# A fused attention and feed-forward kernel: the fourth chunk's tokens are transposed on TensorE in place of the DMA, and the weight scaling and the attention ranks move with it

## The chip, the cores and the metric

The kernel runs on one core of one Trainium2 chip. The metric is device time in microseconds (us) of one execution. Before the change three runs took 210.88, 211.31 and 212.09 us; the median is 211.31 us.

## What is computed

Attention with a window of 128 tokens and 4 always visible first tokens (sinks), over 4 batches, 8 heads, 768 tokens and 64 values per head. The heads are put side by side into tokens of 512 values, and a feed-forward layer with a norm and a residual follows.

```python
scores = scale * np.matmul(q, k.transpose(0, 1, 3, 2))
keep = is_sink | in_window            # first 4 keys, or 0 <= i - j < 128
a = softmax(np.where(keep, scores, -1e9))
x = np.matmul(a, v)                   # heads side by side: (4, 768, 512)
xn = (x - mu) / np.sqrt(var + 1e-06) * g_ln
out = x + np.maximum(xn @ w_ch1, 0.0) @ w_ch2    # 512 -> 2048 -> 512
```

The inputs and the output are fp32; the kernel multiplies in bf16.

## The kernel before, in words

**Tiles and chunks.** The 3072 tokens are 24 tiles of 128 (t = 0 to 23) and 12 chunks of 256 (c = 0 to 11, two tiles each, three chunks per batch). For each chunk the kernel transposes q and k, computes the attention of its two tiles, normalises the tokens, transposes them (`xnt`) and runs the two layers of the feed-forward part.

**Transposes of q and k** (`chunk`, line 674). Chunks 0 to 3 (`c < by_dma`, 4) are transposed by matmuls with an identity (`by_pairs`, L618 and L625). From chunk 4 on POOL issues loads that cast to bf16 (L724), and SP issues DMA transposes (`dma_t`, L597). Line 727 puts the q transposes of chunk 5 and later behind the DMA transpose, on SP, of the second tile of the chunk two before (`trx_op[2 * c - 3]`), where that transpose exists. `gate` and `gate_v` (lines 590 to 594) hold back POOL's loads of k, q and v from chunk 5 on until a certain tile's norm (`rs_op`) is done.

**Attention.** Chunks 0 to 2 use `attend_tile` and `attend`; from tile 6 on `block(t)` (line 941) is one job of TensorE: the values of tile t-1 (L981, L988, L997) and the scores of tile t (L1008, for an even tile also the sinks, L1016). ACT takes the exponential (L1026, L1036), DVE multiplies by the band of the window (L1031). DVE then divides the values by the softmax sum (L1049, L1051).

**Norm** (`normalise`, line 899). DVE: mean and variance (L902, L904). POOL: variance plus 1e-6, to the power -0.5, two instructions (L912, L913). In chunks 0 to 2 `xc` is x minus the mean (L909, waits for no POOL result; the factor is put in at the end). From chunk 3 on (`by_seven`) `xc` is also multiplied by POOL's result (L916), so it waits for it. Then the tokens are transposed. For chunks below `x_by_dma` (3) TensorE transposes, four matmuls per tile into one PSUM bank (L924), and DVE or ACT moves them out and multiplies by the norm's weight g (L935, or four instructions on ACT, L936). From chunk `x_by_dma` on SP issues one DMA transpose per tile (L926, L597), and g has to be in w1 already.

**The scaling of w1** (lines 1260 to 1268). Behind the first layer of chunk `x_by_dma - 1` the four slices of w1 are multiplied by g in place: 16 instructions, on DVE (L1266) or ACT (L1267). Each waits for the last matmul that uses the unscaled slice (`last_use`), and the first layer of later chunks waits for the scaled slice (`Bw1g`, line 1071).

**Feed-forward** (`mlp`, line 1056). The first layer is eight jobs of 8 matmuls (L1067), each followed by a relu (L1078 on ACT, L1080 on DVE). The second layer is a plain product for chunks 0 to 2 (`second`, L1214). From chunk 3 on `second_by_seven` (line 1087) makes it from seven products instead of eight: DVE forms sums of relu results (L1095), TensorE multiplies (L1118), ACT copies parts out (L1125) and frees the bank that the next product writes, DVE adds up (L1129, L1159).

**What sets the order.** Nothing is written in order by hand. Each job is given to a planner (`Plan`) with its engines and cost in us, its rank (`prio`), and what it reads and writes. `Plan.run` (line 116) goes through time: of the jobs whose start lies within a window of the earliest possible start on that engine (0.3 us on TensorE, 0.25 on ACT, DVE and POOL), it takes the one of lowest rank. The result is one fixed order per engine, in which the chip waits for semaphores. Costs that matter here: POOL's two norm instructions 0.88 us; scaling one piece of w1 0.26 us on DVE and 0.065 + 0.000833 x 512 = 0.49 us on ACT; from one engine to another 0.035 us, to TensorE 0.11. `lat` (line 108) adds a lateness from `PAR["late"]` where TensorE waits for a DMA of a given name, if it is planned behind 30 us.

**Ranks.** First layer of chunk c: 16c + 8.5 to 16c + 15.5. Second layer: from 16c + 16.5 on. Block t of chunk c: `d = at(c, "blk") + step * i - lead[min(c, 5)]` with `at(c, "blk")` = 16c - 16 and i = 0 or 1 (line 943). TensorE transposes of tokens: 16c + 1 + i. So before the change block 6 ranks 30, block 7 40, block 8 43, block 9 53, block 10 55 (its values, a job of its own, 51), block 11 65.

Of the kernel before, what the change touches and what calls it, by code (L numbers as in the profile page):

```python
# [65 lines left out]
class Plan:  # L66
# [41 lines left out]
    def lat(self, src, dst):  # L108
        if src.eng == "PE" and src.dma is None:
            return -self.PE_DRAIN if dst == "PE" else self.SEM  # L110
        late = PAR["late"].get(src.name[:3], 0.0) if src.dma is not None and src.start > 30.0 and dst == "PE" else 0.0
        return late + (self.TO_PE if dst == "PE" else self.SEM)

    WINDOW = {"PE": 0.3, "ACT": 0.25, "DVE": 0.25, "POOL": 0.25, "SP": 0.0}

    def run(self):
# [8 lines left out]
        while ready:  # L125
# [4 lines left out]
            for o in ready:  # L130
                if "PE" in o.engs and o is not head and o.prio >= PAR["strict"]:
                    continue
# [66 lines left out]
def pe(us):  # L199
    return {"PE": (us, us + Plan.PE_DRAIN)}  # L200
# [7 lines left out]
def dve(n, per=1.04):  # L208
    t = 0.067 + 0.001 * per * n
    return (t, t + 0.09)  # L210


def fix(occ, extra=0.09):
    return (occ, occ + extra)
# [18 lines left out]
NEVER = -1e9  # L233
BIG = 3.3e38

PAR = dict(late={"trx": 1.25, "trk": 2.0, "trq": 2.0}, solo={10: 4.0}, bh=12, k_nb={(5, "k", 0): 53.0, (5, "k", 1): 53.0, (5, "q", 0): 53.0, (5, "q", 1): 53.0}, vs1=33.0, s4=2.0, w2t_pool=0, cut=(1, 2), rs_nb={4: 48.0, 5: 48.0}, v_nb={8: 49.0, 9: 52.0}, last7=1, opool=0, gk=(5, 4), gv=(4, 5), strict=400.0, win=0.4, tr=-8.0, sc=-5.0, sc1=-2.0, av=2.0, blk=-8.0, step=10.0, trx=9.0, by_dma=4, x_by_dma=3,
           w1p=(1.6, 2.6, 2.7, 2.8), pm=3, w2p=(4.5, 4.51, 4.52, 4.53), apart=2, vs0=(2.0, 13.0), by_tile=0, vp=(0.0, 0.1, 2.0, 2.1, 4.55, 4.56), ld1=0.05, t0=0.8, warm=7.9, pm0=-40.0, w1g=17.0, gtt=1.25, seven=3, lead=(0, 0, 0, 2, 5, 9), w2t=-4.0, at7=(0.5, 1.5, 2.5, 3.5, 4.5, 6.5, 7.5))


def general(tc, nc, slots, pairs, ones, ident_f, ident, w1, w2, mhalf, g_s, g_r, q, k, v, out, scale):  # L240
# [133 lines left out]
def kernel(  # L374
# [24 lines left out]
    NC = B * RC  # L399
# [70 lines left out]
    def constant(name, eng, us, prio, emit, reads=(), **kw):  # L470
        return P.op(name, {eng: fix(us)}, prio, emit, reads=[Bc[r] for r in reads], **kw)
# [46 lines left out]
    def negs(e):  # L518
# [27 lines left out]
    for b in range(B):  # L546
        n_vs = 4 if b else H
        P.op(f"vs{b}", {"DVE": dve(260)} if b else {"POOL": (0.9, 1.0)}, PAR["vs0"][0] if b == 0 else PAR["vs1"] - 12 if b == 1 else 48.0 * b - 20, lambda e, b=b, n=n_vs: (V if b else G).tensor_tensor(
            vs[b], vc[:, b, :].unsqueeze(1).to_broadcast([128, n, 65]),
# [21 lines left out]
    def at(c, step):  # L571
        return 16.0 * c - 8.0 + PAR[step]
# [11 lines left out]
    def early(t):  # L584
        return 0.5 + 0.8 * t

    rs_op, trx_op = {}, {}
    natf_users, natp_users = [], []

    def gate(c):  # L590
        return [rs_op[2 * c - PAR['gk'][c > 5]]] if PAR["by_dma"] < c < NC else []

    def gate_v(c):
        return [rs_op[2 * c - PAR['gv'][c != 5]]] if PAR["by_dma"] < c <= NC else []

    def dma_t(dst, src):
        nc.sync.dma_start_transpose(out=dst, in_=src)  # L597
# [54 lines left out]
    def load_m(t, prio):  # L652
        b, r = min(t, NT - 1) // RB, t % RB
        m = vn_b[t] = Buf(f"v{t}", "vn")
        at = lambda t0, s0, n, hs: v[t0, hs, s0:s0 + n, :].rearrange("h p d -> p h d")
        lo, hi, s0 = slice(0, 4), slice(4, 8), 128 * r
        parts = []
        if r:
            parts = [(0, 128, hi, at(b, s0 - 64, 128, hi)), (0, 64, lo, at(b, s0, 64, lo)), (64, 64, lo, at(b, s0 - 64, 64, lo))]
        else:  # L660
            pb = (t - 1) // RB
            parts = [(0, 64, hi, at(pb, S - 64, 64, hi)), (64, 64, lo, at(pb, S - 64, 64, lo))]
            if t < NT:
                parts += [(64, 64, hi, at(b, 0, 64, hi)), (0, 64, lo, at(b, 0, 64, lo))]
        for i, (p0, n, hs, src) in enumerate(parts):
            P.op(f"vld{t}_{i}", {"POOL": (0.8, 0.85)}, prio + 0.001 * i, lambda e, p0=p0, n=n, hs=hs, src=src: G.dma_start(  # L666
                m.t[p0:p0 + n, hs, 0:64], src), writes=[m], dma=SW_H if n == 128 else SW_Q, after=list(ones_of.values()) + gate_v(t // 2), nb=PAR["v_nb"].get(t, 0.0))
# [6 lines left out]
    def chunk(c):  # L674
        b, R = c // RC, c % RC
        d = at(c, "tr") if c >= 2 else early(2 * c)
        ld = d - 14.0 if c >= RC else 4.0
        if c < 2:
            kT_b[c], qT_b[c] = Buf(f"kT{c}", "kT"), Buf(f"qT{c}", "qT")
            if c == 0:  # L680
                nats = [Buf("kf", "natf"), Buf("qf", "natf")]
                for hh in range(2):
                    hs = slice(4 * hh, 4 * hh + 4)
                    for i, (x, T) in enumerate(((k, kT_b[c]), (q, qT_b[c]))):
                        nm, src, part = "kq"[i], nats[i], Buf(f"{'kq'[i]}l{hh}")
                        ap = x[b, hs, 0:256, :].rearrange("h (p i) d -> p h (i d)", i=2)
                        P.op(f"{nm}ld{hh}", {("SP" if i == 0 else "ACT"): (0.53, 0.53)}, -70 + hh,
                             lambda e, src=src, ap=ap, hs=hs: (nc.sync if e == "SP" else nc.scalar).dma_start(
                                 src.t[:, hs].rearrange("p h i d -> p h (i d)"), ap), writes=[src, part], dma=HW_F)
# [558 lines left out]
    w2t = [[flat_f[0][:, m] for m in range(2)], [flat_f[1][:, m] for m in range(2)], flat_p[0:2], flat_p[2:4]]  # L1248
# [114 lines left out]
```

## Time and profile before

| | |
|---|---|
| Median of three runs | 211.31 us (210.88 to 212.09) |
| The profiled execution, its own time | 210.67 us |
| Its span, first to last instruction | 209.2 us |
| Mean granted TensorE clock | 0.997 of full speed |
| DMA | 27.82 MB in 104557 packets, mean 133 GB/s |

In the profile PE is TensorE's matmuls, PEld its weight loads, DVE VectorE, ACT ScalarE, POOL GpSimd and SP SyncE; SPq and POOLq are the queues that issue DMAs. A group's line has the source line, the engine, the operation, output and input tile, the shapes and the count; behind the bar stand the busy time in us, the mean of one in ns, and the idle time of the engine just before, with what ended it. A line of a timeline has start and length in us. Matmuls overlap, so the time that one costs is read from the start of the next group and not from its own length. Since TensorE works through one fixed order, its idle time in a stretch, and what ended it, is the first thing to look for.

### The profile page before, as it was taken

The page shows a single profiled execution, that of the slowest core. Times are in us where ns is not written, and L with a number is a line of the kernel's source. Part 1 is how long each engine was busy: PE and PEld are TensorE (multiplying, and loading weights), DVE is VectorE, ACT ScalarE, POOL GpSimd, SP SyncE. Part 2 cuts the span into 40 slices and gives each one's busy share as a digit, 9 for nine tenths or more (in the row PEclk, how much of TensorE's full clock was granted, in tenths as well). Part 3 has the DMA queues.
Part 4 walks back from the last instruction along what each step waited for, and adds up shares of the span by engine and source line. Part 5 has one row for each costly group of instructions (what it writes and reads, how often), then busy time and mean ns, then how long its engine had stood idle before and what let it go on. Part 6 is the DMA issues. An engine that isn't in the chain of part 4 may idle for free.

```text
span 209.2 us, 7213 instructions
## 1 busy us (share of the span) xinstructions
PE 201.6 (96%) x2969; PEld 170.0 (81%) x2971; DVE 158.5 (76%) x427; ACT 122.2 (58%) x214; POOL 116.2 (56%) x170
## 2 busy tenths in 40 slices
PE   7899999999999799999999999999999999999992
PEld 2558865688888688888888888888888888888881
DVE  5699865899897778787778788778778678673472
ACT  3798677153897176385665664665664764453610
POOL 7969842479989974757694693694632202410000
PEclk9999999999999999999999999999999999999998
DMA  5999999999999999999999999999992220220202
GB/s 154 191 186 200 190 208 203 171 180 130 151 184 133 144 170 135 120 207 127 100 153 155 109 135 161 132 154 143 145 173 51 78 75 5 81 73 0 103 25 85
DMA packets 104557, 27.82 MB, mean 133 GB/s; under 512 B 93764, under 2 KB 101576, under 8 KB 104520
## 3 DMA queue, kind: packets, MB, share of 16 engines
q0 software_dynamic: 70960, 13.18, 92.1%
q1 hardware_dynamic: 32360, 13.35, 38.9%
q10 hardware_dynamic: 1200, 0.79, 1.3%
q8 instruction: 24, 0.39, 0.9%
q14 instruction: 13, 0.11, 0.2%
HBM read 27.43 MB, written 6.29 MB: 161 GB/s over the span
## 4 chain that ended last, share of the span: by engine, by line
PE 86%; DMA 5%; DVE 3%; ACT 2%; issue 1%; POOL 1%; ACTq 0%; DVEq 0%
PE one L1067 40%; PE one L1118 27%; PE one L1214 7%; DMA xnt<-xc 3%; PE pair L1008 3%; DMA natf<-in_q_dram 3%; PE one L981 2%; PE one L988 2%; PE one L997 1%; DVE st L902 1%; PE pair L1016 1%; ACT qT L671 1%; PE one L924 1%; DVE x L894 1%; PE pair L751 1%
## 5 line engine op out<-in xcount | busy, mean ns | idle before, releaser
L1067 PE MATMUL one<-xnt,w 128*128 128x256 bf16 x768 | 88.7, 273 | 1.1 <-DMA xnt<-xc 1.1
L1067 PEld LDWEIGHTS <-w 128*128 128x128 bf16 x768 | 74.2, 98 | 10.6 <-DMA xnt<-xc 1.4
L1078 ACT ACTIVATE h<-one 128x512 bf16<-128x512 f32 x90 | 53.6, 599 | 37.1 <-PE one L1067 36.4
L666 POOL DMA_DIRECT2D vn<-in_v_dram x59 | 39.2, 689 | 8.7 <-DMA w<-in_moe_w_ch_dram 7.3
L912 POOL TENSOR_SCALAR st<-st 128x1 f32<-128x1 f32 x24 | 9.5, 396 | 48.1 <-DVE st L904 47.5
L1026 ACT ACTIVATE pe<-pair 128x768 bf16<-128x768 f32 x36 | 27.2, 808 | 11.8 <-PE pair L1008 11.8
L1118 PEld LDWEIGHTS <-h 128*128 128x128 bf16 x216 | 20.7, 98 | 2.8
L1214 PE MATMUL one<-w,h 128*128 128x256 bf16 (+1 forms) x158 | 22.4, 293 | 0.2
L1125 ACT COPY tx<-one 128x256 f32<-128x256 f32 x24 | 8.9, 372 | 18.5 <-PE one L1118 18.5
L1214 PEld LDWEIGHTS <-h 128*128 128x128 bf16 x160 | 15.3, 98 | 4.8 <-DMA w<-in_moe_w_ch_dram 0.4
L1118 PE MATMUL one<-w,h 128*128 128x256 bf16 x144 | 18.7, 273 | 0.0
L1118 PEld LDWEIGHTS <-sb 128*128 128x128 bf16 x176 | 16.9, 98 | 2.2
L913 POOL TENSOR_TENSOR st<-st,mhalf 128x1 f32<-128x1 f32 x24 | 17.1, 711 | 2.0
L902 DVE BATCH_NORM_STATS2 st<-x 128x6 f32<-128x512 bf16 x24 | 16.7, 694 | 0.8
L1051 DVE TENSOR_TENSOR x<-one,rec 128x256 bf16<-128x256 f32 x36 | 15.3, 425 | 1.2
L1159 DVE TENSOR_TENSOR ot<-ot,x 128x512 f32<-128x512 f32 x15 | 10.4, 692 | 7.6 <-ACT ot L1125 7.4
L724 POOL DMA_DIRECT2D nat<-in_k_dram x16 | 14.9, 935 | 1.4 <-DMA natp<-in_q_dram 1.4
L724 POOL DMA_DIRECT2D nat<-in_q_dram x16 | 14.2, 903 | 0.0
L916 DVE TENSOR_SCALAR xc<-x,st 128x512 bf16<-128x512 bf16 x18 | 7.8, 431 | 8.2 <-POOL st L913 8.2
L1118 PE MATMUL one<-natf,sb 128*128 128x256 bf16 x92 | 12.5, 273 | 0.0
L1031 DVE TENSOR_TENSOR pe<-pe,band 128x768 bf16<-128x768 bf16 x24 | 12.1, 541 | 0.2
L1118 PEld LDWEIGHTS <-natc 128*128 128x128 bf16 x112 | 10.7, 98 | 1.5
(148 smaller groups left out, 300.0 us busy)
## 6 DMA issues: line engine op xcount, KB each, us to landing
out_dram<-ot SPq DMA_DIRECT2D x22, 256.0 KB
w<-in_moe_w_ch_dram POOLq DMA_DIRECT2D x6, 512.0 KB, 12.9
nat<-in_k_dram POOLq DMA_DIRECT2D x16, 128.0 KB, 4.6
nat<-in_q_dram POOLq DMA_DIRECT2D x16, 128.0 KB, 6.0
vn<-in_v_dram POOLq DMA_DIRECT2D x44, 32.0 KB, 5.3
w<-in_moe_w_ch_dram POOLq DMA_DIRECT2D x4, 256.0 KB, 11.1
vn<-in_v_dram POOLq DMA_DIRECT2D x15, 64.0 KB, 5.2
natp<-in_k_dram POOLq DMA_DIRECT2D x3, 256.0 KB, 10.6
```

Of the source, the lines that this page charges most:

```text
L666: P.op(f"vld{t}_{i}", {"POOL": (0.8, 0.85)}, prio + 0.001 * i, lambda e, p0=p0, n=n, hs=hs, src=src: G.dma_start(m.t[p0:p0 + n, hs, 0:64], ...
L724: lambda e, nat=nat, ap=ap: G.dma_start(nat.t, ap), writes=[nat], dma=SW_N, after=gate(c), nb=PAR["k_nb"].get((c, nm, i), 0.0))
L902: P.op(f"bn{t}", {"DVE": fix(0.60)}, d + 0.12, lambda e: V.bn_stats(st.t[:, 8:14], x.t), reads=[x], writes=[st, mv])
L913: G.tensor_tensor(st.t[:, 16:17], st.t[:, 17:18], mhalf, op=ALU.pow)),
L1026: nc.scalar.activation(pes[j].t.rearrange("p a b -> p (a b)")[:, 0:768].rearrange("p (a b) -> p a b", a=2), pps[j].t[:, :, 0:384], AF.Exp, ...
L1031: V.tensor_mul(at_s, at_s, band[j] if r > 1 else edge[r][j].unsqueeze(1).to_broadcast([128, 4, 192]))
L1051: P.op(f"x{t - 1}{u}", {"DVE": dve(256)}, d + 0.051 + 0.002 * u, lambda e, u=u, rc=rc, pv=pv: V.tensor_tensor(x.t[:, 256 * u:256 * u + 256 ...
L1067: nc.tensor.matmul(ph.t[:, 256 * s:256 * s + 256], lhsT=w1[ht // 4][:, j, 128 * (ht % 4):128 * (ht % 4 + 1)], rhs=xnt.t[:, j, :], start=j ...
L1078: nc.scalar.activation(dst, ph.t, AF.Relu)
L1118: nc.tensor.matmul(bank.t[:, 0:256], lhsT=left[p](m)[:, a, :], rhs=right[p](m)[:, a, :], start=new and m + a == 0, stop=m + a == 4, skip_g ...
L1159: V if e == "DVE" else G).tensor_tensor(ot[i].t, ot[i].t, x.t, op=ALU.add), reads=[ot[i], *oo[i], x], writes=[done])
L1214: nc.tensor.matmul(pc.t[:, part], lhsT=h1[s].t[:, 256 * ii + 128 * i:256 * ii + 128 * i + 128], rhs=w2[s][:, ii, sl.start + part.start:sl. ...
```

## The change

`x_by_dma` goes from 3 to 4. With it:

- The two tiles of chunk 3 (the fourth chunk) are transposed by TensorE and moved out with a multiplication by g; SP's two DMA transposes of them are gone, and with them the entry that line 727 looks up for chunk 5's q.
- w1 is scaled behind the first layer of chunk 3, not of chunk 2 (rank 65 and up in place of 49 and up).
- `step` goes from 10 to 9 and `lead` from (0, 0, 0, 2, 5, 9) to (0, 0, 0, 0, 5, 8): block 6 ranks 32, 7 41, 8 43, 9 52, 10 56 (its values 52), 11 65; of the later blocks the even ones rank one later, the odd ones the same.
- `late` becomes 2.5 us for the DMA transposes of tokens, k and q (from 1.25, 2.0 and 2.0), 0.5 for the loads of w2 (from none), and holds at all times, not only behind 30 us.
- `gate` and `gate_v` have 4 in place of `by_dma`, which is 4; `slack` is empty, and `tr4` is added for chunk 4 only where `by_dma` is above 4.

```diff
     def lat(self, src, dst):
         if src.eng == "PE" and src.dma is None:
             return -self.PE_DRAIN if dst == "PE" else self.SEM
-        late = PAR["late"].get(src.name[:3], 0.0) if src.dma is not None and src.start > 30.0 and dst == "PE" else 0.0
-        return late + (self.TO_PE if dst == "PE" else self.SEM)
+        late = PAR["late"].get(src.name[:3], 0.0) if src.dma is not None and dst == "PE" else 0.0
+        slack = PAR["slack"].get(src.eng, 0.0) if src.dma is None and dst == "PE" and src.start > 24.0 else 0.0
+        return late + slack + (self.TO_PE if dst == "PE" else self.SEM)
...
-PAR = dict(late={"trx": 1.25, "trk": 2.0, "trq": 2.0},
+PAR = dict(tr4=0.0, slack={}, late={"trx": 2.5, "trk": 2.5, "trq": 2.5, "w2l": 0.5},
...
-    step=10.0, by_dma=4, x_by_dma=3, lead=(0, 0, 0, 2, 5, 9)
+    step=9.0, by_dma=4, x_by_dma=4, lead=(0,0,0,0,5,8)
...
     def gate(c):
-        return [rs_op[2 * c - PAR['gk'][c > 5]]] if PAR["by_dma"] < c < NC else []
+        return [rs_op[2 * c - PAR['gk'][c > 5]]] if 4 < c < NC else []
 
     def gate_v(c):
-        return [rs_op[2 * c - PAR['gv'][c != 5]]] if PAR["by_dma"] < c <= NC else []
+        return [rs_op[2 * c - PAR['gv'][c != 5]]] if 4 < c <= NC else []
...
+        if c == 4 and c < PAR["by_dma"]:
+            d += PAR["tr4"]
```

More of the change, by code (lines that the diff above doesn't have):

```diff
@@ L234 @@
 BIG = 3.3e38
-PAR = dict(late={"trx": 1.25, "trk": 2.0, "trq": 2.0}, solo={10: 4.0}, bh=12, k_nb={(5, "k", 0): 53.0, (5, "k", 1): 53.0, (5, "q", 0): 53.0, (5, "q", 1): 53.0}, vs1=33.0, s4=2.0, w2t_pool=0, cut=(1, 2), rs_nb={4: 48.0, 5: 48.0}, v_nb={8: 49.0, 9: 52.0}, last7=1, opool=0, gk=(5, 4), gv=(4, 5), strict=400.0, win=0.4, tr=-8.0, sc=-5.0, sc1=-2.0, av=2.0, blk=-8.0, step=10.0, trx=9.0, by_dma=4, x_by_dma=3,
-           w1p=(1.6, 2.6, 2.7, 2.8), pm=3, w2p=(4.5, 4.51, 4.52, 4.53), apart=2, vs0=(2.0, 13.0), by_tile=0, vp=(0.0, 0.1, 2.0, 2.1, 4.55, 4.56), ld1=0.05, t0=0.8, warm=7.9, pm0=-40.0, w1g=17.0, gtt=1.25, seven=3, lead=(0, 0, 0, 2, 5, 9), w2t=-4.0, at7=(0.5, 1.5, 2.5, 3.5, 4.5, 6.5, 7.5))
+PAR = dict(tr4=0.0, slack={}, late={"trx": 2.5, "trk": 2.5, "trq": 2.5, "w2l": 0.5}, solo={10:4.0}, bh=12, k_nb={(5, "k", 0): 53.0, (5, "k", 1): 53.0, (5, "q", 0): 53.0, (5, "q", 1): 53.0}, vs1=33.0, s4=2.0, w2t_pool=0, cut=(1, 2), rs_nb={4: 48.0, 5: 48.0}, v_nb={8: 49.0, 9: 52.0}, last7=1, opool=0, gk=(5, 4), gv=(4, 5), strict=400.0, win=0.4, tr=-8.0, sc=-5.0, sc1=-2.0, av=2.0, blk=-8.0, step=9.0, trx=9.0, by_dma=4, x_by_dma=4,
+           w1p=(1.6, 2.6, 2.7, 2.8), pm=3, w2p=(4.5, 4.51, 4.52, 4.53), apart=2, vs0=(2.0, 13.0), by_tile=0, vp=(0.0, 0.1, 2.0, 2.1, 4.55, 4.56), ld1=0.05, t0=0.8, warm=7.9, pm0=-40.0, w1g=17.0, gtt=1.25, seven=3, lead=(0,0,0,0,5,8), w2t=-4.0, at7=(0.5, 1.5, 2.5, 3.5, 4.5, 6.5, 7.5))
 def general(tc, nc, slots, pairs, ones, ident_f, ident, w1, w2, mhalf, g_s, g_r, q, k, v, out, scale):
```

## The prediction

> **What bounds the kernel now.** I read the page's summary of engines first, then the table of busy time by stretches, then TensorE's own waits.
>
> ```profile
> PE 201.6 (96%) x2969; PEld 170.0 (81%) x2971; DVE 158.5 (76%) x427; ACT 122.2 (58%) x214; POOL 116.2 (56%) x170
> ```
> ```profile
> 0.00:10.00 10.00, 7.91 (x61) 4.23 (x63) 5.55 (x29) 5.38 (x9) 8.82 (x16) 1.00 1.16 173
> 10.00:20.00 10.00, 9.59 (x195) 7.04 (x190) 9.34 (x26) 9.01 (x15) 7.96 (x13) 1.00 1.60 192
> ...
> 55.00:60.00 5.00, 5.00 (x102) 4.48 (x103) 4.50 (x11) 5.00 (x10) 4.64 (x8) 1.00 1.99 176
> 60.00:65.00 5.00, 5.00 (x57) 4.40 (x54) 4.40 (x14) 5.00 (x9) 4.03 (x7) 1.00 1.89 128
> 65.00:70.00 5.00, 4.27 (x90) 3.58 (x87) 4.10 (x11) 1.55 (x3) 4.81 (x9) 1.00 1.92 113
> 70.00:75.00 5.00, 4.65 (x88) 4.00 (x92) 3.05 (x9) 2.02 (x4) 3.93 (x6) 1.00 1.69 197
> ...
> 100.00:120.00 20.00, 20.00 (x348) 17.75 (x347) 15.34 (x41) 12.52 (x24) 13.22 (x19) 1.00 1.74 133
> ...
> 200.00:209.20 9.20, 5.42 (x50) 4.56 (x48) 4.74 (x14) 0.19 (x1) 0.00 (x0) 0.93 0.18 62
> ```
> ```profile
> PE one L1067 <- DMA xnt<-xc: 1.1, 1, 1.1
> ...
> PE one L924 <- DVE xc L909: 0.4, 1, 0.4
> ```
>
> Columns of the stretches: length, then busy time of PE, PEld, DVE, ACT, POOL, the granted clock, DMA. TensorE is the bound. Of 209.2 us it is idle for 7.6: 2.5 in the first 20 us (start), 3.8 behind 200 us (the last sums and stores), and 1.08 in the middle, in the two stretches around 70 us; from 75 to 200 us it has no idle time at all, at a clock of 1.00. So a change can gain only by taking work from TensorE or by that one hole, and each instruction it adds to TensorE shows in full. Now the hole, on TensorE and along the chain of work that ended last:
>
> ```profile
> 66.48 2.79 PE L1214 MATMUL one<-w,h 128*128 128x256 bf16 x24
> 70.35 1.05 PE L1067 MATMUL one<-xnt,w 128*128 128x256 bf16 x8 [1.08 <-DMA xnt<-xc]
> ```
> ```profile
> 61.13 0.18 DVE rec L1049
> ...
> 62.53 0.19 DVE st L904
> 62.80 0.44 POOL st L912
> 63.32 0.74 POOL st L913
> ...
> 64.52 5.79 DMA xnt<-xc
> ```
>
> Chunk 2's second layer (L1214) is used up at 69.27, and the first layer of the fourth chunk (chunk 3, L1067) starts only when its tokens come back transposed from the DMA, 5.79 us after issue. Nothing else was ready.
>
> **The change, step by step.**
>
> *The hole goes: -1.08 us.* In place of the DMA stand four PE transposes per tile and one eviction with the weight multiplied in. The same operations of chunks 0 to 2 give the price:
>
> ```profile
> 44.70 0.40 PE L924 MATMUL one<-ident,xc 128*128 128x128 bf16 x4
> 44.94 1.04 PE L1214 MATMUL one<-w,h 128*128 128x256 bf16 x8
> 45.81 0.39 PE L924 MATMUL one<-ident,xc 128*128 128x128 bf16 x4
> 46.03 1.04 PE L1214 MATMUL one<-w,h 128*128 128x256 bf16 x8
> ```
> ```profile
> L935 DVE TENSOR_TENSOR xnt<-one,gt 128x512 bf16<-128x512 bf16 x5 | 3.3, 686 | 0.8 <-PE one L924 0.7
> ```
>
> xc of tile 7 is there at 64.52; with 0.4 for the transposes and 0.69 for the eviction, chunk 3's input is complete near 65.6, or 66.5 if the values of tile 7 come one unit of chunk 2's first layer later (8 matmuls; 44.94 to 45.81 above is 0.87). TensorE arrives there at 69.27 plus what is added: over 2.5 us of room. What would be late next? Of the two conditions left, the scaled w1 is no longer needed by this layer, and the second half of the queries of chunk 5 (below) is needed only by block 10:
>
> ```profile
> 74.67 0.54 PE L1008 MATMUL pair<-qT,kT 64*64 64x128 bf16 x32
> ```
>
> *The transposes: +0.46 us.* Starts 44.70 to 44.94 and 45.81 to 46.03: 0.24 and 0.22 of TensorE's time for four each, all of it on the path, since TensorE has no idle time to hide it in. One by itself is longer, and only their overlap makes it 0.06:
>
> ```profile
> L924 PE MATMUL one<-ident,xc 128*128 128x128 bf16 x24 | 2.3, 220 | 0.4 <-DVE xc L909 0.4
> ```
>
> The Trainium skill, page "TensorE: Matmul & The Clock Gate", section "Part 4: PE-mode transpose", speaks against the small figure: about 275 ns for one transpose in a kernel's context, and that the full clock does not engage in this mode. By it the eight would cost 2.2 us, an estimate from that page, and the sum would be +1.4. The trace agrees with that page on the length of one (220 ns), and not on the cost of four in a row (0.24 us).
>
> *A wait of TensorE for xc: +0.30 us.* The chunk's xc needs the POOL result first (L916), unlike that of chunks 0 to 2 (L909). The planner that writes the order counts 0.88 us for the two POOL instructions and 0.035 on either side, 0.95. The rows above have 62.72 (62.53 + 0.19) for the end of L904, and this one the start of L916:
>
> ```profile
> 64.08 0.41 DVE L916 TENSOR_SCALAR xc<-x,st 128x512 bf16<-128x512 bf16 x1 [0.47 <-POOL st L913]
> ```
>
> That is 1.36, so the transpose may stand in TensorE's queue up to 0.41 us before its data. Behind it are queued chunk 2's second layer and block 9, and they wait with it. Tile 6 hardly suffers: its transposes rank 49, behind chunk 2's first layer (40.5 to 47.5), so they come late anyway. For tile 7 (rank 50) pieces of 0.87 us stand around it, and the planner takes a job up to 0.3 us ahead of its time: with an evenly spread phase the mean of what is left is 0.72 x 0.72 / 2 / 0.87 = 0.30. Bounds: 0 and 0.8 (both tiles). The nearest row is the 0.4 that L924 waited once in six times for L909.
>
> *The evictions: 0.* Two of 0.69 on DVE between 57 and 66 us. They lie beside TensorE's 5.00 of 5.00, and DVE and ACT lose the scaling from this stretch. Without that cover they would still have the 2.5 us of room.
>
> *w1's scaling moves some 16 us later: 0, and up to +2.0.* Sixteen instructions:
>
> ```profile
> L1267 ACT ACTIVATE w<-w,gt 128x512 bf16<-128x512 bf16 x10 | 6.6, 734 | 0.0
> ...
> L1266 DVE TENSOR_SCALAR w<-w,gt 128x512 bf16<-128x512 bf16 x6 | 2.3, 414 | 0.0
> ```
> ```profile
> 57.88 3.17 ACT L1267 ACTIVATE w<-w,gt 128x512 bf16<-128x512 bf16 x5
> ```
>
> They now run between 55 and 65 us, where ACT is 5.00 of 5.00 busy, and TensorE lost nothing there. Behind the change they start when chunk 3's first layer has used a slice (from 71 us) and must be done, slice by slice, for chunk 4's first layer, whose bulk begins at 88.91:
>
> ```profile
> 88.91 5.35 PE one L1067 x48
> ```
>
> From 70 to 75 ACT is busy for 2.02 of 5.00 and DVE for 3.05, so there is room. The danger is the seven products of chunk 3 behind 79 us. The planner counts 0.49 us for a scaling on ACT and 0.26 on DVE; five in a row took 3.17, 0.63 each, and DVE's mean is 0.41. If both engines are packed, they run late by 10 x 0.14 + 6 x 0.1 = 2.0. I take 0, by the stretch 55 to 65, and keep 2.0.
>
> *The order: 0, between -0.4 and +0.5.* Ranks of the attention blocks: 6 from 30 to 32, 7 from 40 to 41, 9 from 53 to 52, 10 from 55 to 56 (its values from 51 to 52), 8 the same, from chunk 5 on the even ones one later and the odd ones the same. Block 6 stays ahead of rank 32.5 where it now runs; block 7 goes behind one unit of chunk 2's first layer; the others move by at most one 0.87-us unit within a stream that has no gaps, so the sum stays. The DMA transposes' lateness in the plan grows to 2.5 and w2's to 0.5; this only places the instructions that need them later. A pessimistic plan costs where nothing else is ready, one piece of half a product (4 matmuls, 0.44); a better one saves at most this wait for w2:
>
> ```profile
> PEld L1214 <- DMA w<-in_moe_w_ch_dram: 0.4, 1, 0.4
> ```
>
> *Queues: 0.* SP loses two issues of a transpose:
>
> ```profile
> 64.52 1.19 SPq L597 DMA_TRANSPOSE xnt<-xc  x1
> 65.88 1.19 SPq L597 DMA_TRANSPOSE qT<-nat  x1
> ...
> 67.86 2.37 SPq L597 DMA_TRANSPOSE qT<-nat  x1
> ```
>
> The two qT of chunk 5 stood behind the second xnt by an explicit order (line 727), which falls away because that transpose no longer exists; they can go earlier. Their user, block 10, had no wait, so nothing is won, but this is the next DMA that would have been late. POOL's loads are gated as before (4 is the old value), so POOL's queue keeps its order but for the ranks; `tr4` and `slack` do nothing at these values.
>
> Sum: -1.08 + 0.46 + 0.30 = -0.32 us. The profiled execution took 210.67 us (span 209.2 and 1.5 around it), which gives 210.35; the median of the runs shown is 0.64 above it, 211.31, and becomes **211.0 us**.
>
> **The rivals.**
>
> *A, the hole was larger than the profiled one.* The runs shown reach from 210.88 to 212.09, and the only wait of TensorE for a DMA in mid-kernel is the one at 70 us: if it is what makes the median 0.64 longer than the profiled run, all of this goes too, and the wait for xc is covered: 211.31 - 1.08 - 0.64 + 0.46 = 210.05. For it: a transfer of 5.79 us in a busy stretch may vary. Against it: the start and the stores vary as well.
>
> *B, ACT and DVE become the bound of chunk 3's products, slower.* A product that reuses a bank waits for ACT's copy out of it:
>
> ```profile
> 82.75 0.37 ACT L1125 COPY tx<-one 128x256 f32<-128x256 f32 x1 [0.46 <-PE one L1118]
> ```
> ```profile
> 82.55 1.04 PE L1118 MATMUL one<-w,h 128*128 128x256 bf16 x8
> 83.42 1.04 PE L1118 MATMUL one<-natf,sb 128*128 128x256 bf16 x8
> ```
>
> The copy ends at 83.12 and the product that needs the bank starts at 83.42: 0.3 us of room. With the whole 2.0 of lateness 1.7 reach TensorE: 211.31 - 0.32 + 1.7 = 212.7. It decides (over 0.5%) from 1.4 us of lost time. For it: relu, exponentials, copies and scaling all meet on two engines between 72 and 88 us. Against it: the same load left TensorE at 5.00 of 5.00 from 55 to 65.
>
> *C, the wait only moves.* Chunk 4's input is now the first to come by DMA, issued at 76.46 here and used at 84.30 without a wait. If TensorE comes earlier and the transfers do not, 1.08 is paid there again: 211.31 + 0.46 = 211.8, or 212.1 with the wait for xc.
>
> ```profile
> 76.46 1.22 SPq L597 DMA_TRANSPOSE xnt<-xc  x1
> ```
> ```profile
> 84.30 1.04 PE L1067 MATMUL one<-xnt,w 128*128 128x256 bf16 x8
> ```
>
> *D, the transposes do not overlap* and cost their 220 ns each: 211.31 - 1.08 + 8 x 0.22 + 0.30 = 212.3. Against it: the two rows with 0.24 and 0.22 for four. The page named above would have it so, at its own figure.
>
> **How the numbers follow.** Chances: forecast 0.44, A 0.27, B 0.19, C 0.08, D 0.02. A measurement of this kernel can tell about 0.5%, 1.06 us, from no change: faster is below 210.25, slower above 212.37. The forecast's own range, with xc's wait from 0 to 0.8 and the order from -0.4 to +0.5, is 210.3 to 212.0. A is faster but for a few of its cases (0.25), and the lowest of the forecast's adds 0.03; B is slower but for its mild cases (0.17), and D, C and the upper end of the forecast add 0.05. So faster 0.28, slower 0.22, same 0.50. The range for 8 in 10 takes in most of A and B: 209.8 to 212.6.
>
> **What would show it.** The hole: no idle time of TensorE between 65 and 75 us, and L924 with 32 matmuls. The xc step: a wait of L924 for L916 of about 0.3. The scaling: L1266 and L1267 between 71 and 90 us; B if the products of chunk 3 (L1118) show idle time there with ACT or DVE as releaser. C if L1067 waits for xnt at chunk 4. A if the runs of the changed kernel lie closer together. The forecast is wrong if TensorE's idle time from 75 to 200 us is no longer zero, or if the start before 30 us moves by more than 0.4.

## The result, and the profile after

| | before | after |
|---|---|---|
| Median (20 runs each) | 211.22 us (210.22 to 213.24) | 210.25 us (209.80 to 211.78) |
| Ratio, with its 95% interval | | 0.9957 [0.9939, 0.9974] |
| The profiled execution, its own time | 210.67 us | 210.53 us |
| Its span | 209.2 us | 209.0 us |
| Mean granted TensorE clock | 0.997 | 1.00 |

The kernel is faster by 0.43%, between 0.26 and 0.61%: 0.91 us, between 0.55 and 1.29. The interval ends below 1, so the gain is clear of the noise; it is also within the 0.5% that the prediction counted as "same". In the lines of after, most line numbers are three higher than before (L924 is now L927, L1067 is L1070, L1118 is L1121, L1214 is L1217, L1266 and L1267 are L1269 and L1270, L909 and L916 are L912 and L919, L597 is L598).

The waits of TensorE in after:

```profile
PE one L703 <- ACT natc L695: 1.3, 3, 0.6
...
PE one L927 <- DVE xc L912: 0.8, 2, 0.4
```

No wait for `xnt` is left. The table of busy time by stretches, of after (length, then PE, PEld, DVE, ACT, POOL, clock, DMA):

```profile
60.00:65.00 5.00, 5.00 (x107) 4.42 (x105) 3.31 (x9) 3.55 (x9) 4.59 (x8) 1.00 2.79 127
65.00:70.00 5.00, 5.00 (x101) 4.50 (x99) 4.17 (x11) 1.51 (x2) 3.87 (x7) 1.00 1.80 163
70.00:75.00 5.00, 5.00 (x105) 4.39 (x103) 4.22 (x11) 3.78 (x7) 4.84 (x8) 1.00 1.04 105
```

The two stretches around 70 us, 4.27 and 4.65 before, are 5.00 and 5.00: the hole is closed, and from 60 to 200 us TensorE has no idle time. The timeline of TensorE in after, around 44 us and around the fourth chunk:

```profile
43.01 1.04 PE L1217 MATMUL one<-w,h 128*128 128x256 bf16 x8
44.39 0.40 PE L927 MATMUL one<-ident,xc 128*128 128x128 bf16 x4 [0.35 <-DVE xc L912]
...
62.37 0.39 PE L927 MATMUL one<-ident,xc 128*128 128x128 bf16 x4
62.59 2.78 PE L1217 MATMUL one<-w,h 128*128 128x256 bf16 x24
65.21 0.39 PE L927 MATMUL one<-ident,xc 128*128 128x128 bf16 x4
65.43 0.41 PE L984 MATMUL one<-vn,pe 128*128 128x65 bf16 x8
...
66.48 3.67 PE L1217 MATMUL one<-w,h 128*128 128x256 bf16 x32
69.99 0.41 PE L984 MATMUL one<-vn,pe 128*128 128x65 bf16 x8
...
70.59 0.52 PE L1011 MATMUL pair<-qT,kT 64*64 64x128 bf16 x32
...
71.27 7.16 PE L1070 MATMUL one<-xnt,w 128*128 128x256 bf16 x64
```

Four things are to be seen. The transposes of chunk 3 (62.37 and 65.21) cost 0.22 us each: that is how much later the next group starts. There is no wait at them. And behind chunk 2's second layer (L1217 at 66.48) stands the whole block 10, its values at 69.99 and its scores at 70.59, *ahead* of chunk 3's first layer (71.27). Before, the scores of block 10 came at 74.67, behind half of that layer. The input of that layer does not need this: DVE's last move out of PSUM, in the first row below, ends at 66.08 + 0.68 = 66.76, over 3 us before TensorE comes to block 10. The second row, of SP's queue, bears on block 10:

```profile
66.08 0.68 DVE L938 TENSOR_TENSOR xnt<-one,gt 128x512 bf16<-128x512 bf16 x1
```
```profile
61.47 3.42 SPq L598 DMA_TRANSPOSE qT<-nat  x2
```

The two q transposes of chunk 5, which block 10's scores need, are issued at 61.47, in place of 65.88 and 67.86. Line 727 had held them behind a token transpose that no longer exists.

One new piece of idle time has come in, 0.35 us at 44.39. It is a wait for `xc` of tile 4 in chunk 2 (L912), whose own work the change does not touch.

**A measure for the middle.** The start differs by some tenths from one execution to the next, so I also read from each trace the time between two rows that both kernels have: the first 24 matmuls of chunk 0's first layer that stand in one piece, and the scores of the last block. For before and for after:

```profile
20.84 2.78 PE L1067 MATMUL one<-xnt,w 128*128 128x256 bf16 x24
...
172.45 0.52 PE L1008 MATMUL pair<-qT,kT 64*64 64x128 bf16 x32
```
```profile
21.00 2.78 PE L1070 MATMUL one<-xnt,w 128*128 128x256 bf16 x24
...
172.09 0.52 PE L1011 MATMUL pair<-qT,kT 64*64 64x128 bf16 x32
```

That is 151.61 before and 151.09 after, 0.52 less, though the profiled executions as wholes differ by only 0.14. Two executions of one kernel differ by up to 0.20 in this measure (table below), and each kernel of an experiment has only one, so smaller differences say nothing.

### The profile page after: what moved, and what is told of

It is laid out like the page before. It is cut to its first block, busy times and chain, and to the rows that moved or that the text cites. A ratio compares the mean times of both kernels' runs of the same rounds, so it can differ in the third digit from the quotient of the medians.

```text
span 209.0 us, 7235 instructions
## 1 busy us (share of the span) xinstructions
PE 201.2 (96%) x2979; PEld 169.6 (81%) x2979; DVE 161.1 (77%) x433; ACT 120.8 (58%) x216; POOL 115.9 (55%) x170
## 4 chain that ended last, share of the span: by engine, by line
PE 89%; DVE 4%; DMA 3%; ACT 1%; issue 1%; ACTq 0%; DVEq 0%
PE one L1070 40%; PE one L1121 27%; PE one L1217 10%; PE pair L1011 3%; DMA natf<-in_q_dram 3%; PE one L984 2%; PE one L991 2%; PE one L1000 1%; DVE st L905 1%; DVE x L897 1%; PE one L927 1%; PE pair L1019 1%; DVE xc L912 1%; PE pair L626 1%; PE pair L754 1%
## 5 line engine op out<-in xcount | busy, mean ns | idle before, releaser
L1070 PE MATMUL one<-xnt,w 128*128 128x256 bf16 x768 | 88.6, 273 | 0.1
L1070 PEld LDWEIGHTS <-w 128*128 128x128 bf16 x768 | 73.9, 98 | 10.0 <-issue 0.3
L1081 ACT ACTIVATE h<-one 128x512 bf16<-128x512 f32 x86 | 51.3, 598 | 35.8 <-PE one L1070 33.6
L1121 PEld LDWEIGHTS <-h 128*128 128x128 bf16 x216 | 21.1, 98 | 2.6 <-issue 0.2
L1217 PE MATMUL one<-w,h 128*128 128x256 bf16 (+1 forms) x160 | 22.9, 294 | 0.0
L1217 PEld LDWEIGHTS <-h 128*128 128x128 bf16 x160 | 15.1, 98 | 4.6
L1121 PEld LDWEIGHTS <-sb 128*128 128x128 bf16 x176 | 16.9, 98 | 2.3
L1121 PE MATMUL one<-w,h 128*128 128x256 bf16 x144 | 18.7, 273 | 0.0
L1128 ACT COPY tx<-one 128x256 f32<-128x256 f32 x24 | 9.0, 375 | 16.1 <-PE one L1121 16.1
L916 POOL TENSOR_TENSOR st<-st,mhalf 128x1 f32<-128x1 f32 x24 | 16.5, 687 | 2.0
L919 DVE TENSOR_SCALAR xc<-x,st 128x512 bf16<-128x512 bf16 x18 | 7.4, 413 | 7.5 <-POOL st L916 7.5
L1121 PE MATMUL one<-natf,sb 128*128 128x256 bf16 x92 | 12.5, 272 | 0.0
L1121 PEld LDWEIGHTS <-natc 128*128 128x128 bf16 x112 | 10.7, 98 | 1.4
```

The source lines that it names most:

```text
L916: G.tensor_tensor(st.t[:, 16:17], st.t[:, 17:18], mhalf, op=ALU.pow)),
L1070: nc.tensor.matmul(ph.t[:, 256 * s:256 * s + 256], lhsT=w1[ht // 4][:, j, 128 * (ht % 4):128 * (ht % 4 + 1)], rhs=xnt.t[:, j, :], start=j ...
L1081: nc.scalar.activation(dst, ph.t, AF.Relu)
L1121: nc.tensor.matmul(bank.t[:, 0:256], lhsT=left[p](m)[:, a, :], rhs=right[p](m)[:, a, :], start=new and m + a == 0, stop=m + a == 4, skip_g ...
L1217: nc.tensor.matmul(pc.t[:, part], lhsT=h1[s].t[:, 256 * ii + 128 * i:256 * ii + 128 * i + 128], rhs=w2[s][:, ii, sl.start + part.start:sl. ...
```

## The experiments

Theory: the hole at 70 us is what goes, and the transposes on TensorE remove it. First rival: the new order (ranks and lateness) closes it without them. Second rival: the move of w1's scaling decides, as a cost in chunk 3's products or as a relief where it stood. "Middle" is the measure just given.

| Kernel | Middle, us | Median, us | Ratio to before [interval] |
|---|---|---|---|
| before (three profiles) | 151.61, 151.81, 151.75 | 210.98 to 211.22 | |
| after (two profiles) | 151.09, 150.93 | 210.25; 210.36 | 0.9957 [0.9939, 0.9974]; 0.9967 [0.9947, 0.9987] |
| e1, transposes only | 151.19 | 210.52 | 0.998 [0.9962, 0.9999] |
| e2, order only | 150.89 | 210.37 | 0.9978 [0.9952, 1.0003] |
| e3, scaling stays | 151.15 | 210.91 | 0.9993 [0.9979, 1.0006] |
| e4, slack for DVE | 151.66 | 211.25 | 1.0007 [0.9991, 1.0023] |
| e5, lateness only | 150.84 | 210.41 | 0.9974 [0.9954, 0.9994] |
| e6, ranks only | 151.40 | 210.09 | 0.9974 [0.9949, 0.9998] |
| e7, dearer scaling in the plan | 152.05 | 211.88 | 1.0043 [1.0022, 1.0063] |
| e8, transposes twice | 151.27 | 210.48 | 0.9968 [0.995, 0.9987] |
| e9, ranks and transposes | 150.53 | 210.18 | 0.9964 [0.9948, 0.9979] |

**e1: the transposes alone.** The kernel before, with one value changed.

```diff
-    x_by_dma=3
+    x_by_dma=4
```

> The kernel before with x_by_dma 4 and nothing else: TensorE transposes the fourth chunk and w1 is scaled behind it, ranks and latenesses as before. Theory (the gain is the hole at the fourth chunk's first layer, less the transposes): 0.5 to 0.9 us under before, no wait of the first layer for xnt between 60 and 76 us, eight transposes more. Rival 1 (the gain comes from ranks and latenesses): 0.4 us over before or no change, since only the transposes' 0.46 us is added. Rival 2 (the scaling's new place makes the gain): as the theory.

The hole is gone here too; the middle is 151.19, 0.5 less than the mean of before. But the scaling has a price in this order. The timeline of TensorE in e1, then ACT's:

```profile
69.85 0.54 PE L1008 MATMUL pair<-qT,kT 64*64 64x128 bf16 x32
...
85.09 0.60 PE L1118 MATMUL one<-w,sb 128*128 128x256 bf16 x4 [0.19 <-ACT tx L1125]
```
```profile
82.76 2.02 ACT L1267 ACTIVATE w<-w,gt 128x512 bf16<-128x512 bf16 x3
84.61 0.43 ACT L1125 COPY tx<-one 128x256 f32<-128x256 f32 x1
```

Three scalings in a row (2.02 us) delay the copy that frees a bank, and a product waits for it: it starts 1.23 us after the group before it (at 83.86), where eight matmuls take 0.87, and one product earlier 0.18 is lost in the same way of counting. This is the mechanism of rival B, at about a quarter of its price. The first row shows that block 10's scores go ahead of chunk 3's first layer (71.27) in e1 too, with the old ranks and lateness: it is not the new order that moves them.

**e2: the order alone.** The kernel after, with the tokens of chunk 3 still transposed by DMA, so that only ranks and lateness are new.

```diff
-    x_by_dma=4
+    x_by_dma=3
```

> The kernel after with x_by_dma back at 3: only ranks and latenesses are changed. Theory: within 0.3 us of before, the wait for xnt at the fourth chunk's first layer still there (0.7 to 1.5 us). Rival 1: 0.9 us or more under before, the wait gone, since nothing is paid for transposes. Rival 2: no change.

No wait for `xnt` was there, though the DMA transpose is; this contradicts the expectation of 0.7 to 1.5 us. The timeline of TensorE, in before and then in e2:

```profile
71.24 0.41 PE L981 MATMUL one<-vn,pe 128*128 128x65 bf16 x8
```
```profile
66.37 3.65 PE L1217 MATMUL one<-w,h 128*128 128x256 bf16 x32 [0.59 <-issue]
69.86 0.41 PE L984 MATMUL one<-vn,pe 128*128 128x65 bf16 x8
...
70.56 3.67 PE L1070 MATMUL one<-xnt,w 128*128 128x256 bf16 x32
```

The values at 69.86 now stand between chunk 2's second layer and chunk 3's first (before, they came at 71.24, behind the layer's first eight matmuls), and the layer starts at 70.56 without a wait. So the order by itself removes the wait at the layer; that the hole needs the transposes to go does not hold. But there is a wait of 0.59 at 66.37 instead. Without it TensorE would have come to the layer that much earlier, at 69.97, when the tokens may not have been there; so a part of the hole may only have moved. DVE's timeline in e2:

```profile
57.96 3.71 DVE L1269 TENSOR_SCALAR w<-w,gt 128x512 bf16<-128x512 bf16 x10
...
65.42 0.74 DVE L1226 SCALAR_TENSOR_TENSOR ot<-one,st,x 128x512 f32<-128x512 f32 x1
```

Ten scalings in a row hold DVE until 61.67; the norm behind them is late, and the sum (L1226) that empties a bank of the second layer ends at 66.16, just before TensorE goes on. The name "issue" in the wait shows no semaphore; that the bank is the reason is read from these times alone.

**e3: the scaling stays where it was.** The kernel after, but w1 is scaled behind chunk 2. Since chunk 3 then multiplies by the scaled w1, the move out of PSUM leaves out the multiplication by g for that chunk.

```diff
-        if c == PAR["x_by_dma"] - 1:
+        if c == 2:
...
-  reads=[xnt, Bw1g[u // 2] if c >= PAR["x_by_dma"] else ...
+  reads=[xnt, Bw1g[u // 2] if c >= 3 else ...
...
+            (V.tensor_copy if e == "DVE" else nc.scalar.copy)(dst(), src()) if c == 3 else
```

> The kernel after, but w1 is scaled behind the third chunk as before, and the fourth chunk's tokens are moved out of PSUM without the weight. Theory: within 0.3 us of the kernel after (some 0.9 under before), since the input of the fourth chunk has over 2.5 us of room and the scaling never held TensorE. Rival 2: 0.3 us or more slower than the kernel after, with a wait at the fourth chunk's first layer or its transposes. Should the small waits of the fourth chunk's products (85.4 to 85.7 us in the profile after) come from the moved scaling, they are gone here, worth 0.2 us.

The timelines of TensorE and of DVE in e3:

```profile
62.19 2.78 PE L1218 MATMUL one<-w,h 128*128 128x256 bf16 x24
65.63 0.40 PE L927 MATMUL one<-ident,xc 128*128 128x128 bf16 x4 [0.66 <-DVE xc L919]
```
```profile
58.03 3.71 DVE L1270 TENSOR_SCALAR w<-w,gt 128x512 bf16<-128x512 bf16 x10
...
65.16 0.41 DVE L919 TENSOR_SCALAR xc<-x,st 128x512 bf16<-128x512 bf16 x1 [0.47 <-POOL st L916]
```

Here is the wait for `xc` that the prediction priced at 0.30. It exists, and is larger (0.66), when the scaling keeps DVE from the norm: `xc` of tile 7 starts at 65.16, against 64.60 in after. The two small delays that after has in chunk 3's products (see below) are gone. So moving the scaling is not only a risk: it keeps the transposes from waiting. The runs go further than the trace: e3 cannot be told from before (0.9993), although the profiled execution, 210.52, is the fastest of its twelve, with a median of 210.91. So the expectation, within 0.3 us of after, was not met.

**e4: a more careful plan.** The kernel after, with 0.4 us more in the plan wherever TensorE waits for DVE behind 24 us, meant to remove the wait at 44.39.

```diff
-    slack={}
+    slack={"DVE": 0.4}
```

> The kernel after with slack 0.4 us from DVE to TensorE in the plan: TensorE's jobs that need DVE are planned 0.4 us later. Theory: the wait of the transposes of tile 4 at 44.4 us (0.35 us) goes, 0.2 to 0.4 under the kernel after (some 1.2 under before), if the pessimism costs nothing elsewhere. Rival: the more cautious order leaves TensorE without work in the seven products, so it is no faster, or slower than the kernel after, with idle time behind 80 us.

The wait at 44.39 is gone. The timeline of TensorE in e4 shows what came in its place:

```profile
69.48 1.04 PE L1070 MATMUL one<-xnt,w 128*128 128x256 bf16 x8
...
84.62 1.05 PE L1070 MATMUL one<-xnt,w 128*128 128x256 bf16 x8 [1.27 <-DMA xnt<-xc]
```

TensorE reaches chunk 4's first layer before its tokens: the hole of the kernel before, one chunk later. This is rival C, in a kernel that I made, and it eats the whole gain. The first row tells something about after as well: here chunk 3's first layer begins ahead of block 10, at 69.48, and does not wait. So with the transposes on TensorE the early input is enough to close the hole, without block 10 in front of it.

**Two more profiles of before.** They ask how large the hole is from one execution to the next.

> The kernel before, unchanged, profiled again. Theory (what makes the median 0.6 us longer than the first profiled run is the DMA transfer in front of the fourth chunk's first layer): TensorE's wait for xnt at 70 us differs from the first profile's 1.1 us, and the time less this wait is 209.6 us within 0.2. Rival: the wait is 1.1 us again and a difference in time lies at the start, the end, or in small waits elsewhere.

> The kernel before, unchanged, profiled a third time. Expected as for the look before it: theory, the time less the wait for xnt is 209.6 us within 0.2; rival, the wait is 1.1 us each time and other places vary.

The waits of TensorE in the first and in the second:

```profile
PE one L1067 <- DMA xnt<-xc: 1.3, 1, 1.3
```
```profile
PE one L700 <- ACT natc L692: 1.4, 3, 0.6
...
PE one L1067 <- DMA xnt<-xc: 1.2, 1, 1.2
```

So the profiled hole of 1.08 was the smallest of three. The times less the hole are 210.67 - 1.1 = 209.6, 211.03 - 1.3 = 209.7 and 211.22 - 1.2 = 210.0: the hole takes part in the spread, and the start (L700, 0.4, 0.3 and 1.4) as well. The last value lies outside the 0.2 that was expected.

**e5 and e6: lateness alone, ranks alone.** Each is the kernel before with one half of the new order: e5 has the new `late`, used at all times, and e6 the new `step` and `lead`.

```diff
-        late = ... if src.dma is not None and src.start > 30.0 and dst == "PE" else 0.0
+        late = ... if src.dma is not None and dst == "PE" else 0.0
...
-PAR = dict(late={"trx": 1.25, "trk": 2.0, "trq": 2.0}
+PAR = dict(late={"trx": 2.5, "trk": 2.5, "trq": 2.5, "w2l": 0.5}
```
```diff
-    step=10.0 ... lead=(0, 0, 0, 2, 5, 9)
+    step=9.0 ... lead=(0, 0, 0, 0, 5, 8)
```

> The kernel before with the new latenesses of DMAs in the plan and nothing else. If the latenesses closed the hole in the run with ranks and latenesses alone (a planned wait lets the planner put block 10 and values of tile 9 in front of the fourth chunk's first layer): 0.5 to 0.8 us under before and no wait for xnt behind 60 us. If it was the ranks: no change (within 0.2 us), the wait for xnt near 70 us still there.

> The kernel before with the new step and lead and nothing else. If the ranks closed the hole: 0.5 to 0.8 us under before, no wait for xnt behind 60 us. If it was the latenesses: no change, or up to 0.5 us slower, since the values of tile 7, on which xnt of the fourth chunk depends, come up to 0.9 us later.

The timelines of TensorE in e5 and in e6:

```profile
69.51 0.62 PE L981 MATMUL one<-vn,pe 128*128 128x65 bf16 x8
...
70.78 3.44 PE L1067 MATMUL one<-xnt,w 128*128 128x256 bf16 x30 [0.29 <-DMA xnt<-xc]
```
```profile
69.40 0.43 PE L981 MATMUL one<-vn,pe 128*128 128x65 bf16 x8
...
71.09 3.11 PE L1067 MATMUL one<-xnt,w 128*128 128x256 bf16 x27 [0.90 <-DMA xnt<-xc]
```

Either half moves the same values in front of the waiting layer. In e5 that leaves 0.29 of the hole, in e6 0.90: there TensorE has come to the values nearly half a us earlier than in e2 (69.40 against 69.86), and the tokens come at 71.09, where e2 has them by 70.56. The parts do not add up: e5 and e6 take 0.88 and 0.32 off the middle of 151.72, and the two together, e2, take 0.83. The profiled execution of e6 is not typical, though: it took 210.73, against a median of 210.09. By the medians e5, e6 and e2 take 0.67, 0.99 and 0.70 off the before of their comparison, so which half does more is open; that they do not add up is seen both ways.

**A second profile of after.** It asks whether the wait at 44.39 is chance.

> The kernel after, unchanged, beside the next three on one chip. Theory: 0.8 to 1.0 us under before (hole of 1.25 to 1.5 us as the gap between two matmuls, less 0.46 for the transposes), no wait of TensorE between 44 and 200 us above 0.2 us: the wait of 0.35 us for xc of tile 4 in the first profile was a stretched DVE instruction of that execution and does not come again. Rival: that wait is part of the planned order and is there again.

It came again. TensorE's timeline in the second profile:

```profile
44.38 0.40 PE L927 MATMUL one<-ident,xc 128*128 128x128 bf16 x4 [0.30 <-DVE xc L912]
```

**e7: the scaling at its true price.** The kernel after, with the plan's cost of one scaling raised to what the trace shows, to see whether an honest plan does better.

```diff
-  P.op(f"w1g{s}{j}", {"DVE": fix(0.26), "ACT": act(512)}, ...
+  P.op(f"w1g{s}{j}", {"DVE": fix(0.37), "ACT": fix(0.63, 0.105)}, ...
```

> The kernel after, with the scaling of one piece of w1 entered in the plan at what the trace shows (0.63 us on ACT, 0.37 on DVE, in place of 0.49 and 0.26). If the small waits of the fourth chunk's products (0.16 us at 85.4 us in the profile after, 0.36 us where only the transposes were moved) come from a plan that is too short for the scaling: they go, and the time is 0.1 to 0.3 us under the kernel after. Rival: they come from something else, or the longer plan moves work badly, and the time is the same within 0.1 us or longer.

It is slower by 1.5 us than after in the same comparison (1.0043 against 0.9967). The timelines of TensorE and of ACT in e7:

```profile
84.89 1.05 PE L1121 MATMUL one<-w,natc 128*128 128x256 bf16 x8 [0.61 <-DVE natc L1098]
...
99.85 1.04 PE L1121 MATMUL one<-w,sb 128*128 128x256 bf16 x8 [0.46 <-ACT tx L1128]
```
```profile
81.16 3.18 ACT L1270 ACTIVATE w<-w,gt 128x512 bf16<-128x512 bf16 x5
```

The plan now gives ACT 13 scalings in place of 9, five of them in a row in the middle of chunk 3's products; DVE has to make copies there that ACT makes in after (L1128, at 81.88 and 84.08), its own sum (L1098) starts only at 84.41, and a product of chunk 3 waits for it, at 84.89. From start to start this product is 0.78 late (1.65 after the group at 83.24, in place of 0.87), and the next 0.12. The second wait, at 99.85, is in a product of chunk 4, 14 us behind the last scaling, and what the scaling has to do with it is not shown. The first is rival B in its place, with ACT packed and DVE taking over its work. After and e7 scale the same 16 pieces, so it was the order of the scalings that decided the cost, not the room as such.

**e8: the transposes twice.** The kernel after, with chunk 3's transposes issued a second time into the same place.

```diff
-            for j in range(NDM):
+            for j in 2 * list(range(NDM)) if c == 3 else range(NDM):
```

> The kernel after, with each of the eight added transposes issued twice (the second writes the same values again). Theory: a set of eight costs 0.46 us of TensorE's time, all of it in the total: 0.4 to 0.5 over the kernel after. Rival (transposes do not overlap): 1.8 us over. Rival (they are hidden in waits): within 0.1 us.

The timeline of TensorE in e8:

```profile
62.44 0.61 PE L927 MATMUL one<-ident,xc 128*128 128x128 bf16 x8
62.88 2.78 PE L1217 MATMUL one<-w,h 128*128 128x256 bf16 x24
65.50 0.61 PE L927 MATMUL one<-ident,xc 128*128 128x128 bf16 x8
65.95 0.41 PE L984 MATMUL one<-vn,pe 128*128 128x65 bf16 x8
```

Eight take 0.44 and 0.45 where four took 0.22: one transpose costs 0.055 us of TensorE's time in a row. The eight added ones are 0.45 us on the spot. At the last scores 0.34 of it is left (151.27 against 150.93), and the medians differ by only 0.12, which the intervals cannot tell from 0 or from 0.45. So the cost on the spot is shown, and that all of it reaches the total is not.

**e9: ranks and transposes, with the old lateness.**

```diff
-    step=10.0, ... x_by_dma=3, lead=(0, 0, 0, 2, 5, 9)
+    step=9.0, ... x_by_dma=4, lead=(0, 0, 0, 0, 5, 8)
```

> The kernel before with the new step, lead and x_by_dma 4; latenesses as before. The ranks alone and the latenesses alone each gave 0.26%, the transposes alone 0.2%, and ranks with latenesses 0.22%. Theory (all of them remove the same hole, so that they do not add up): 0.5 to 1.0 us under before, as the kernel after within 0.3 us. Rival (they add up, since each has a gain of its own): without the latenesses 0.5 us slower than the kernel after.

It has the shortest middle of all, 150.53, and no wait at 44 us. Its ratio, 0.9964, is that of after in the same comparison, 0.9967: by the medians the new lateness is not needed, and no version better than the changed kernel can be told apart.

## Why the prediction was right, point by point

The forecast was 211.0 us, no change beyond 0.5%, with a small gain; 210.25 was measured, within 209.8 to 212.6, but just below the forecast's own range, which began at 210.3. The sum was -0.32; measured were -0.91 (-0.55 to -1.29).

- **The hole goes, -1.08.** The mechanism was right (the input is complete at 66.76, and e4 starts the layer at 69.48 without a wait); the term was too small. Behind the 24 matmuls that start at 66.48 in before, the next could start at 66.48 + 24 x 0.11 = 69.12 (32 of them take 3.51 in after, 66.48 to 69.99, so 0.11 each); it started at 70.35. The hole is thus 1.23 us, where the idle column gives 1.08 because it counts from the modelled end of the last matmul. In the other two profiles of before it is 1.51 and 1.35, counted in the same way (66.58 to 70.72 and 66.82 to 70.80, less 2.63).
- **The transposes, +0.46.** Measured 0.44 (0.22 + 0.22), and 0.45 for the second set in e8. Rival D is refuted, and with it, as a cost in a row, the price of 275 ns each that the Trainium skill states in "TensorE: Matmul & The Clock Gate", section "Part 4: PE-mode transpose": 0.055 us here, at a granted clock of 1.00 throughout these stretches. The length of one, 220 ns, is nearer to that page's figure but below it.
- **A wait for xc, +0.30.** This step failed: there is none at chunk 3. The 1.36 us from the norm to `xc` was right (1.38 in after), but the mean over all moments at which the transposes' turn may come did not come true: the lower bound, 0, did. `xc` is ready at 64.60 + 0.41 = 65.01, and the turn comes at 65.21; e1 and e8 have no wait there either, and e9 0.15 from start to start. The working of this term left out that the change also clears DVE of the scalings between 58 and 62 us, in front of this norm: with them e3 has 0.66.
- **The evictions (the moves out of PSUM), 0.** Right: TensorE is at 5.00 of 5.00 beside them, from 60 to 70 us.
- **The scaling moves, 0 up to +2.0.** Nearly right: 9 on ACT and 7 on DVE, from 74.59 to 84.1. In after, two products of chunk 3 start late, by 0.15 and 0.09. The timeline of TensorE in after:

```profile
81.94 1.04 PE L1121 MATMUL one<-w,h 128*128 128x256 bf16 x8
82.90 1.03 PE L1121 MATMUL one<-natf,sb 128*128 128x256 bf16 x8
...
85.08 0.60 PE L1121 MATMUL one<-w,natc 128*128 128x256 bf16 x4
85.67 1.03 PE L1121 MATMUL one<-natp,h 128*128 128x256 bf16 x8
```

  Eight matmuls take 0.87 and four 0.44; here the next starts 0.96 and 0.59 later. That is rival B, at 0.24, and e3, where the scaling stays, has neither delay. Its upper bound of 2.0 was not reached: e7, the worst, loses 0.9 in the same products. (By its own figures, 0.41 less 0.26, the bound should have counted 0.15 and not 0.1 for a scaling on DVE.)
- **The order, 0 between -0.4 and +0.5.** This step failed in its reasoning. It said that each block moves by one unit at most within a stream without gaps. But the stream had one gap, and work can move into it. In e2, e5 and e6 the values of tile 9 go in front of the waiting layer, from 71.24 to 69.86 and earlier, and the wait shrinks or goes with the transpose still on the DMA. (The scores of block 10 are another matter, see the queues below.) So the hole's term and the order's are one and the same gain, which can be had only once. It also cost something: at 44.39 TensorE lost 43.01 + 0.88 to 44.39, 0.50, of which the trace calls 0.35 idle. The transposes of tile 4 stand there ahead of those of q and k (L626) in the kernels with the new lateness except e4, and behind them in before, e1, e6 and e9, which have no such wait. Nor have e2, e3 and e7, where they stand ahead and the DVE instruction in front of them is quick (last section).
- **w2.** The wait of 0.4 for w2 that the prediction quoted is gone in after, and still there in e6, whose lateness is the old one. Between the starts of the matmuls it cost 0.2 in the first profile of before, and 0.2 and 0 in the other two.
- **What would show it.** There are 32 transposes at L927, TensorE's idle time from 75 to 200 us is still zero, and the start moves by 0.16 (20.84 to 21.00), less than the 0.4 that would have spoken against the forecast. TensorE's idle time in the first 20 us grows from 2.50 to 3.46, but one of the other profiles of before has 3.55.
- **The queues, 0.** Right in that nothing waits for the q transposes. Not seen was what goes with their earlier issue. In after, e1, e3, e8 and e9 they are issued between 61 and 63 us, and block 10's scores stand ahead of chunk 3's first layer; in before, e2, e5 and e6 line 727 holds them until 65.88 or later, and the scores come behind half of that layer (74.16 to 74.67). So the move of the scores goes with the transposes and not with the ranks. No run took line 727's hold away alone.

With the measured sizes the profiled pair gives -1.23 + 0.44 + 0.24 + 0.50 - 0.2 = -0.25, and its middle shows -0.52; the other 0.27 was not traced. That -0.25 lies near the forecast's -0.32 is luck: the 0.30 that did not come is made up by 0.50 and 0.24 that were not in the sum. With the larger hole of the other two profiles the sum is about -0.4, and the mean middle falls from 151.72 to 151.01, 0.71, which is within the interval of the medians. The median before was 0.64 above the profiled execution, and rival A had put all of that down to the hole, for 210.05. The measured 210.25 lies near that price, and the runs do lie closer together: the middle half of them spans 0.4 us after and 1.0 before. But in the comparison with the second profile of after it is 0.3 and 0.4, so this sign is weak. And A's reason is only shown in part: the hole was larger by 0.1 to 0.3 in the two other profiles, not by 0.64. What makes up the remaining half us is open; the waits at the start differ as much (L700 for 0.3 to 1.4 in three profiles of before), and they are not the change's doing. Rival C did not come in the changed kernel, only in e4.

## What to carry to other kernels

A hole in an engine that is otherwise full can be closed by making its input earlier or by putting other ready work in front of it; before pricing the first, look for the second, for the two gains are the same and do not add. Read the size of the hole from start to start and from several executions. When an edit moves work off an engine, price what waited behind that work as well as what will wait at its new place: here the place it left was worth up to 0.66 us, the place it went to cost 0.24, and a plan that only looked more exact (e7) cost 1.5 us against after, one more careful (e4) about 1.

## What the runs showed of the hardware

The wait at 44.39 comes with one DVE instruction that takes twice its time. The timelines of POOL and of DVE in after, then of both in e4, where the same instruction is quick:

```profile
43.35 1.77 POOL L727 DMA_DIRECT2D nat<-in_k_dram  x2 [1.33 <-DMA natp<-in_q_dram]
```
```profile
43.56 0.77 DVE L912 TENSOR_SCALAR xc<-x,st 128x512 bf16<-128x512 bf16 x1
```
```profile
43.40 1.89 POOL L727 DMA_DIRECT2D nat<-in_k_dram  x2 [1.39 <-DMA natp<-in_q_dram]
```
```profile
43.58 0.35 DVE L912 TENSOR_SCALAR xc<-x,st 128x512 bf16<-128x512 bf16 x1
```

It takes 0.35 us when it starts 0.18 us or less behind the start of POOL's DMA issue (e2, e3, e4 and e7: -0.03, 0.13, 0.18 and 0.01), and longer when it starts 0.19 or more behind it (after 0.21, its second profile 0.26, e8 0.19, e5 0.46). In the last four it lasts 0.77, 0.72, 0.79 and 0.53, and ends each time 0.98 or 0.99 us after POOL began (43.56 + 0.77 - 43.35 = 0.98). In before, its other two profiles, e1, e6 and e9 it starts ahead of POOL's issue and takes 0.35. The same instruction of tile 5, 2 to 3 us later, fits in all 14 profiles: nine times it starts 0.18 to 0.49 behind an issue's start, takes 0.52 to 0.84 and ends 1.01 to 1.03 behind it; five times it starts at most 0.11 behind an issue's start, or just ahead of one, and takes 0.35. And in e3 and e4, where DVE started 0.13 and 0.18 behind POOL and was quick, POOL's issue is the longer one, 0.96 and 1.01 us where issues beside it take about 0.89.

An end that hangs on POOL's start and not on DVE's own looks like a hold that POOL takes about 0.2 us into its issue and gives back about 0.63 us into it (0.98 less 0.35). The Trainium skill, page "SBUF — State Buffer", section "Who interferes with whom", states such a rule: VectorE in some forms, `tensor_scalar` among them, and GpSimd share a pair of ports, which the first to come holds for its whole instruction while the other stands still. The times agree with it in that who comes first decides; that the hold lasts for POOL's whole instruction they do not show (one issue takes 0.89 us, and the hold would end after 0.63). That this is the cause is argued, not shown: no run took the two apart on purpose.
